# The first weight chunk is loaded ahead of the first full load of x, and each of the next three one x load earlier

## The chip, the core and the metric

One NeuronCore of a Trainium2 chip runs the whole program. The metric is the device time of one execution in microseconds; lower is better. TensorE multiplies, VectorE and ScalarE work on tiles, GpSimd (POOL) takes some of the elementwise work, and SP's queue issues nearly all transfers between HBM and the on-chip memory.

## The reference

Three steps follow each other on 2 x 3008 tokens of 256 features. All of it is computed to float32 accuracy.

```python
X = np.fft.fft(np.fft.fft(x, axis=1), axis=2).real      # x: 2, 3008, 256
h = X.reshape(6016, 256) @ w_in                         # 256 x 2048, float64
x = np.maximum(h, 0.0) ** 2 @ w_out                     # 2048 x 256
h = x @ w2_in
P = a[0] + a[1]*h + a[2]*h**2 + a[3]*h**3
Q = 1.0 + abs(b[0])*abs(h) + abs(b[1])*h**2
out = P / (Q + 1e-6) @ w2_out
```

## The kernel before

**The Fourier stage.** The length 3008 is split as 64 x 47. A first transform of length 47 runs on TensorE from x, which comes in ten loads: load 0 is a small one on ACT's queue (`x0`), loads 1 to 7 are two transfers of 384 KB each on SP's queue, loads 8 and 9 one transfer each (`X_CH`, `x_load`, L234). `u_mm` (L246) multiplies a load with the constant `c47`, in two halves of the feature axis. Each half goes through the load's first transfer and then through its second. ScalarE copies one half, VectorE adds and subtracts, and the result is the tile U (`u_copy`, `u_out`). When all ten loads are in U, `f_d` and `f_s` transform on (with the constants `cd` and `r0`), and ScalarE and VectorE split the result into x1h and x1l, the high and low parts of a tile of tokens. There are four slots for loads of x (`xt`).

**The weights.** Each layer has 16 chunks of weights. A chunk of the first layer comes as raw float64 words in two transfers of 256 KB (`w_load`, L328). ScalarE takes an absolute value (L337), VectorE puts the float32 together in four steps (L340 to L354), then sums and differences (L361), ScalarE rounds to the high part (L369) and VectorE subtracts to get the low part (L374). Then the first layer's product `h1` can use the chunk. A single row of weights, `w0`, is loaded, split and placed by small steps of its own (L379 to L406).

**The layers.** Twelve tiles of 384 or 512 tokens go through layer one (h1, the relu square, o1) and layer two (h2, the rational function, o2). Each product is three passes of high and low parts. Tiles 0 and 1 go through layer one side by side (`ORDER1`), while their chunks are still being made; from then on tiles follow one another. In the first microseconds and in the Fourier stage some multiplies of zeros (`hot`, L282) run on TensorE for its clock.

**The order of the work.** Every step is entered into a planner, `Queues`, with an engine, an assumed cost, a place, what it needs and which slots it takes. The planner then goes through time: among all steps that are ready it takes the one with the smallest key, and the order that it finds is the program's order on every engine.

```python
rank = (start, op["place"], op["n"])                                         # L110
...
place = -32 + c
...
add(("x", c), "SP" if c else "ACT", 0.54 * n if c else 0.5, place if c else -50, lambda c=c: x_load(c), take=("xt",),
    lat=X_LAT if c > 1 else 4.0 if c else 5.0,
    after=[("wd", W_FIRST[c] - 1)] if W_FIRST[c] else [])                    # L291
...
add(("wd", j), "SP", 1.5, place - 4, lambda j=j, w=w: w_load(j, *w), take=(raw,), lat=DMA_LAT,
    after=([("wd", j - 1)] if j else []) + [("x", c) for c in range(NC) if c < NC and W_FIRST[c] <= j])   # L427
```

`W_FIRST[c]` is the number of weight chunks that stand before load c of x: load c is issued after chunk `W_FIRST[c] - 1`, and chunk j after all loads with `W_FIRST[c] <= j`. Three more steps on SP's queue are tied to loads of x: `w0` is loaded after load 1 and placed after load 6, and `cd` and `r0` have a place (`C_AT`, -21.12) behind the loads of x (-31 and on) and before the chunks (-8 and on), but wait for nothing. `c47` is issued ahead of everything.

Of the kernel before, what the change touches and what calls it, by code (L numbers as in the profile page):

```python
# [52 lines left out]
AB_AT = 0  # L53
W_TAGS = (("g2", "x2h", "g2", "x2l"), ("g2",))
W2_AT, W2_STEP = 6.94, 1.11
W_FIRST, SPILL_W = (0, 0, 1, 1, 2, 2, 3, 3, 4, 4), 16


def f32(ap):
# [962 lines left out]
```

## Time and profile before

| | us |
|---|---|
| runs of the kernel before | 1092.48, 1089.34, 1089.12 (median 1089.34) |
| the profiled execution, its time | 1088.24 |
| its span, first to last instruction | 1086.3 |
| TensorE busy | 1053.5 (97% of the span) |
| VectorE busy | 1009.5 (93%) |
| ScalarE busy | 987.5 (91%) |
| GpSimd busy | 491.7 (45%) |
| mean granted clock of TensorE | 0.996 |

The profile is one execution; its time is the span and 1.9 us around it. Busy shares are means over stages with different limits, so the first 60 us have to be read by themselves. SP's rows are issues of transfers: a transfer's landing is its issue plus the time to landing that the view of transfers gives.

### The profile page before, as it was taken

How to read it: one execution, taken by the hardware profiler on the slowest of the kernel's cores; microseconds unless marked ns; L12 is line 12 of the kernel's file. 1: busy time of each engine (PE TensorE's matmuls, PEld its weight loads, DVE VectorE, ACT ScalarE, POOL GpSimd, SP SyncE). 2: the span in 40 equal slices, each digit the busy share in tenths (PEclk: the TensorE clock that was granted, in tenths of full speed). 3: DMA queues.
4: the chain of work that ended last, by engine and by line, in shares of the span. 5: the costliest groups of instructions: out<-in, count | busy, mean ns of one | idle time of the engine just before them, and what ended most of it. 6: DMA issues, size and time to landing. Idle time of an engine off the chain costs nothing.

```text
span 1086.3 us, 21308 instructions
## 1 busy us (share of the span) xinstructions
PE 1053.5 (97%) x7692; PEld 992.0 (91%) x7692; DVE 1009.5 (93%) x1806; ACT 987.5 (91%) x2009; POOL 491.7 (45%) x373
## 2 busy tenths in 40 slices
PE   9999989999999999999999999999999999999986
PEld 9899978899999999989899989999999999999985
DVE  5999999999899999999899899999899999899997
ACT  3888989999999999989999999999999999999896
POOL 0000015455444555445555545545545555545476
PEclk9999999999999999999999999999999999999999
DMA  9654400000000000000000000000000000000000
GB/s 333 207 204 127 136 1 1 25 2 11 11 11 11 6 16 11 1 21 11 2 21 11 1 21 11 1 21 11 1 21 10 2 11 11 2 11 11 2 11 20
DMA packets 26837, 36.81 MB, mean 34 GB/s; under 512 B 2315, under 2 KB 19341, under 8 KB 26733
## 3 DMA queue, kind: packets, MB, share of 16 engines
q1 hardware_dynamic: 26477, 34.94, 9.6%
q8 instruction: 61, 1.00, 0.4%
q10 hardware_dynamic: 256, 0.52, 0.2%
q14 instruction: 43, 0.35, 0.1%
HBM read 26.65 MB, written 8.78 MB: 33 GB/s over the span
## 4 chain that ended last, share of the span: by engine, by line
PE 51%; ACT 28%; DVE 13%; issue 6%; DMA 2%; POOL 1%; SPq 0%; ACTq 0%; POOLq 0%; DVEq 0%
PE o2a L672 13%; PE p L613 9%; PE o1a L672 6%; PE o1b L672 6%; PE p L644 4%; ACT y L761 4%; PE o2b L613 3%; ACT t L738 3%; ACT g L700 3%; ACT g L706 3%; ACT u L748 3%; ACT y L765 3%; ACT u L733 2%; DVE p L784 2%; ACT g L710 2%
## 5 line engine op out<-in xcount | busy, mean ns | idle before, releaser
L795 POOL TENSOR_TENSOR g<-t,y 128x512 fp32r<-128x512 f32 (+1 forms) x182 | 249.9, 1373 | 423.2 <-DVE t L791 194.8
L715 POOL TENSOR_TENSOR g<-g,g 128x512 fp32r<-128x512 f32 x160 | 211.6, 1323 | 153.8 <-ACT g L710 105.4
L672 PE MATMUL o2a<-g,w2hi 128*128 128x256 f32 (+1 forms) x1440 | 262.8, 283 | 6.8 <-POOL g L795 6.7
L672 PEld LDWEIGHTS o2a<-g,w2hi 128*128 128x128 f32 x1440 | 212.0, 189 | 13.9 <-POOL g L795 9.4
L778 DVE SCALAR_TENSOR_TENSOR g<-t,ab,y 128x512 fp32r<-128x512 f32 (+1 forms) x177 | 137.4, 778 | 13.1 <-ACT y L765 12.0
L672 PE MATMUL o2a<-g,w2lo 128*128 128x256 f32 (+1 forms) x720 | 145.1, 281 | 0.0
L672 PE MATMUL o1a<-g,w1hi 128*128 128x512 f32 x352 | 140.1, 398 | 1.6 <-POOL g L715 1.6
L672 PE MATMUL o1b<-g,w1hi 128*128 128x512 f32 x352 | 138.8, 394 | 0.0
L784 DVE SCALAR_TENSOR_TENSOR p<-u,g 128x512 f32<-128x512 f32 (+2 forms) x178 | 133.3, 749 | 0.7
L791 DVE SCALAR_TENSOR_TENSOR t<-t,ab,p 128x512 f32<-128x512 f32 (+2 forms) x178 | 129.2, 726 | 1.1
L748 ACT ACTIVATE u<-u 128x512 f32<-128x512 f32 (+2 forms) x178 | 110.3, 620 | 13.1 <-DVE u L744 12.3
L613 PE MATMUL p<-x2h,w2hi 128*128 128x256 f32 (+1 forms) x534 | 109.5, 286 | 8.4 <-DVE x1h L789 3.9
L765 ACT ACTIVATE y<-y 128x512 f32<-128x512 f32 (+1 forms) x185 | 115.2, 624 | 1.6
L761 ACT ACTIVATE y<-u 128x512 f32<-128x512 f32 (+1 forms) x177 | 109.6, 620 | 7.4 <-POOL g L795 3.7
L744 DVE SCALAR_TENSOR_TENSOR u<-u,ab,p 128x512 f32<-128x512 f32 (+1 forms) x134 | 97.1, 725 | 19.9 <-ACT t L738 18.9
L700 ACT ACTIVATE g<-g 128x512 f32<-128x512 f32 x160 | 101.2, 633 | 12.9 <-DVE g L690 12.5
L706 ACT ACTIVATE g<-g 128x512 fp32r<-128x512 f32 (+1 forms) x175 | 109.7, 627 | 3.3 <-PE o1b L672 1.9
L672 PEld LDWEIGHTS o2a<-g,w2lo 128*128 128x128 f32 x720 | 111.0, 190 | 0.0
L710 ACT ACTIVATE g<-g 128x512 f32<-128x512 f32 (+1 forms) x175 | 109.6, 626 | 1.2
L613 PE MATMUL p<-x2h,w2lo 128*128 128x256 f32 (+1 forms) x534 | 107.2, 282 | 0.0
L613 PE MATMUL p<-x2l,w2hi 128*128 128x256 f32 (+1 forms) x534 | 107.2, 282 | 0.0
L690 DVE TENSOR_TENSOR g<-p,bc 128x256 f32<-128x256 f32 x238 | 96.6, 417 | 5.5 <-ACT bc L680 3.3
(263 smaller groups left out, 2875.8 us busy)
## 6 DMA issues: line engine op xcount, KB each, us to landing
g<-in_dram SPq DMA_DIRECT2D x48, 256.0 KB, 3.5
xt<-in_dram SPq DMA_DIRECT2D x15, 384.0 KB, 5.8
out_dram<-os SPq DMA_DIRECT2D x21, 256.0 KB, 2.1
udram<-U SPq DMA_DIRECT2D x4, 640.0 KB, 5.3
ut<-udram SPq DMA_DIRECT2D x10, 256.0 KB, 3.0
x2h<-in_dram SPq DMA_DIRECT2D x8, 256.0 KB, 5.2
x2l<-in_dram SPq DMA_DIRECT2D x8, 256.0 KB, 4.4
xt<-in_dram ACTq DMA_DIRECT2D x1, 384.0 KB, 4.8
```

What stands on the lines that cost most here:

```text
L613: nc.tensor.matmul(h[:, c * n:(c + 1) * n], l[:, k, :], r[:, k], start=(q == 0), stop=(q == 5))
L672: nc.tensor.matmul(O[t][e], l[:, e * 128:(e + 1) * 128], r[:, c * n:(c + 1) * n], start=(i == 0 and q == 0 and not one), stop=(i == NF - 1 ...
L700: nc.scalar.activation(out=e["g"], in_=e["g"], func=ACTF.Relu)
L706: nc.scalar.activation(out=e["gh"], in_=e["g"], func=ACTF.Square)
L710: nc.scalar.activation(out=e["g"], in_=e["g"], func=ACTF.Square)
L715: eng.tensor_tensor(out=e["gl"], in0=e["g"], in1=f32(e["gh"]), op=ALU.subtract)
L748: nc.scalar.activation(out=w, in_=w, func=ACTF.Abs)
L761: nc.scalar.activation(out=e["z"], in_=e["w"], func=ACTF.Abs_reciprocal_sqrt, bias=Q1)
L765: nc.scalar.activation(out=z, in_=z, func=ACTF.Square)
L778: nc.vector.scalar_tensor_tensor(out=e["gh"], in0=e["t1"], scalar=a0, in1=e["z"], op0=ALU.add, op1=ALU.mult)
L784: nc.vector.scalar_tensor_tensor(out=e["m"], in0=e["w"], scalar=Q1, in1=f32(e["gh"]), op0=ALU.add, op1=ALU.mult)
L795: nc.gpsimd.tensor_tensor(out=e["gl"], in0=e["t1"], in1=e["z"], op=ALU.mult)
```

## The change

One tuple is edited: the entries of loads 1, 3, 5 and 7 go up by one chunk.

```diff
-W_FIRST, SPILL_W = (0, 0, 1, 1, 2, 2, 3, 3, 4, 4), 16
+W_FIRST, SPILL_W = (0, 1, 1, 2, 2, 3, 3, 4, 4, 4), 16
```

Before, the ties say: loads 0, 1, chunk 0, loads 2, 3, chunk 1, loads 4, 5, chunk 2, loads 6, 7, chunk 3, loads 8, 9, then the other chunks. After, they say: load 0, chunk 0, loads 1, 2, chunk 1, loads 3, 4, chunk 2, loads 5, 6, chunk 3, loads 7, 8, 9, then the other chunks. The planner makes the order of all engines anew from these ties.

## Rows read from the trace of the kernel before

**Rows 1.** The page's table of engines: busy us, share, instructions.
```profile
PE 1053.5 (97%) x7692; PEld 992.0 (91%) x7692; DVE 1009.5 (93%) x1806; ACT 987.5 (91%) x2009; POOL 491.7 (45%) x373
```

**Rows 2.** Stretches: length, busy us (instructions) by engine, TensorE's granted clock, DMA share, GB/s.
```profile
core 0: us, PE busy (x) PEld busy (x) DVE busy (x) ACT busy (x) POOL busy (x), PEclk, DMA share, GB/s
...
8.00:34.00 26.00, 24.58 (x191) 23.92 (x189) 21.97 (x59) 11.30 (x26) 0.00 (x0) 1.00 1.02 363
42.00:56.00 14.00, 12.61 (x93) 11.94 (x92) 13.44 (x35) 12.76 (x36) 0.00 (x0) 1.00 0.29 93
56.00:120.00 64.00, 63.97 (x462) 61.20 (x462) 60.38 (x131) 54.55 (x115) 0.00 (x0) 1.00 0.51 166
```

**Rows 3.** TensorE's waits, 33 to 62 us: total, times, longest.
```profile
PE p L490 <- DVE U L273: 1.3, 1, 1.3
PE p L626 <- ACT y L697: 0.7, 1, 0.7
PE p L626 <- DVE x1l L543: 0.7, 1, 0.7
```

**Rows 4.** Timeline of TensorE: start, us, line, form, count, idle before.
```profile
6.78 1.06 PE L251 MATMUL o1b<-c_t,xt 96*128 96x96 f32 x8
...
11.03 0.59 PE L255 MATMUL p<-c_t,xt 128*128 128x188 f32 x2
...
17.44 0.51 PE L255 MATMUL o2a<-c_t,xt 128*128 128x188 f32 x2
...
20.50 0.51 PE L255 MATMUL p<-c_t,xt 128*128 128x188 f32 x2
...
33.60 0.44 PE L490 MATMUL p<-cd_t,U 128*66 128x130 f32 x2 [1.29 <-DVE U L273]
...
41.97 0.36 PE L626 MATMUL p<-x1h,w1hi 128*128 128x256 f32 x1
```

**Rows 5.** Timeline of SP's queue: start and length of each issue, transfers.
```profile
1.19 0.89 SPq L244 DMA_DIRECT2D xt<-in_dram  x2
...
2.60 0.42 SPq L209 DMA_DIRECT2D cd_t<-in_dram  x1
3.07 0.57 SPq L209 DMA_DIRECT2D r_t<-in_dram  x1
3.68 0.66 SPq L330 DMA_DIRECT2D g<-in_dram  x1
5.50 0.34 SPq L332 DMA_DIRECT2D g<-in_dram  x1
...
13.97 0.33 SPq L332 DMA_DIRECT2D g<-in_dram  x1
```

**Rows 6.** The chain that ended last, in order of time, first pieces: start, us.
```profile
0.74 4.75 DMA xt<-in_dram
5.50 0.34 SPq L332
5.89 5.09 DMA xt<-in_dram
```

**Rows 7.** Transfers issued around 1.9, 3.2, 5.6 and 14 us: KB, us to landing.
```profile
xt<-in_dram SPq DMA_DIRECT2D x1, 384.0 KB, 5.8
...
cd_t<-in_dram SPq DMA_DIRECT2D x1, 257.0 KB, 5.7
r_t<-in_dram SPq DMA_DIRECT2D x1, 66.0 KB
...
g<-in_dram SPq DMA_DIRECT2D x1, 256.0 KB, 4.5
...
g<-in_dram SPq DMA_DIRECT2D x1, 256.0 KB, 8.3
```

**Rows 8.** Timeline of VectorE: its first step on w0, its first on chunk 0.
```profile
8.06 0.21 DVE L392 TENSOR_SCALAR cw<-cw 16x128 f32<-16x128 f32 x1 [7.07 <-ACT cw L383]
...
10.73 0.43 DVE L340 TENSOR_SCALAR cw<-cw 128x512 f32<-128x512 f32 x1 [0.56 <-ACT cw L337]
```

**Rows 9.** Timeline of TensorE, 140 to 151 us: the end of its longest wait.
```profile
144.26 0.61 PE L613 MATMUL p<-x2h,w2hi 128*128 128x384 f32 x2 [2.15 <-DVE t L756]
```

**Rows 10.** Stretch behind that wait, with columns as in rows 2.
```profile
144.00:150.00 6.00, 5.74 (x21) 4.98 (x22) 5.53 (x11) 5.35 (x14) 0.84 (x1) 0.72 0.02 4
```

## The prediction

> **What bounds the kernel now.** I read the page's table of engines first: TensorE is busy 1053.5 of 1086.3 us [rows 1], so over the whole span it is the engine to keep fed, and a change at the start pays only through the moment at which TensorE gets its work and through the holes it has later. The table by stretch tells the stages apart [rows 2]. From 8 to 34 us the 16 DMA engines are full (share 1.02, 363 GB/s), TensorE is busy for 24.58 of 26 us, and VectorE for 21.97, so that it is idle for 26.00 - 21.97 = 4.03 us. From 42 to 56 us the DMA has little to do (share 0.29), VectorE is full (13.44 of 14), and TensorE lacks 14.00 - 12.61 = 1.39 us. From 56 to 120 us TensorE lacks nothing (63.97 of 64).
>
> So the start is a DMA stage in which TensorE is paced by x, followed by a short stage in which VectorE, turning float64 weights into pairs, leaves small holes on TensorE. The table of waits names these: when U is complete TensorE waits 1.3 us for VectorE's last U, and later 0.7 us for ScalarE's y and 0.7 us for VectorE's x1l [rows 3].
>
> The timeline of TensorE shows how close the race of x is [rows 4]: load 0 is finished at 6.78 + 1.06 = 7.84 us, load 2 starts at 11.03, and later one load takes 20.50 - 17.44 = 3.06 us, with no hole between load 4 and load 5. The transform of U starts at 33.60 and the first h1 at 41.97.
>
> **The change part by part.** Only the order of SP's queue is edited, through the planner. Its key is (start, place). With the edit the only loads free at zero are those of the constants, so the planner takes cd and r0 before anything else; then chunk 0 (freed by load 0 on ACT's queue), x load 1, w0, x load 2, chunk 1, loads 3 and 4, chunk 2, loads 5 and 6, the placing of w0, chunk 3, loads 7, 8, 9, chunk 4. No instruction is added or removed. In front of x load 1 come four transfers that were behind it: cd, r0 and the two halves of chunk 0. Later chunk 1 passes load 3, chunk 2 load 5, chunk 3 load 7, two transfers each. From load 8 on the bytes in front of every transfer are as before.
>
> *Issue.* The four took SP 0.42 + 0.57 + 0.66 + 0.34 = 1.99 us [rows 5]. Load 1 was issued from 1.19, so it is now issued from about 3.2. Before, the ninth transfer (chunk 0's second half) was held until 5.50 us, and the chain shows load 0's landing (0.74 + 4.75 = 5.49) in front of it [rows 5, 6]: eight are outstanding at most. Chunk 0 and load 1 are now all within the first eight, and w0 (16 KB) becomes the ninth, issued after 5.50; its steps on VectorE, at 8.06 before [rows 8], come a few us later, into VectorE's idle time. I cost issue and w0 at nothing, since the full DMA engines hide both; without that cover the cost would be 1.99 us, which is less than the next term and inside it.
>
> *Load 1's data.* cd and r0 are 257 + 66 KB and chunk 0 is 2 x 256 KB [rows 7]: 855 kB, 2.36 us at 363 GB/s. Load 1's second half was issued at about 1.19 + 0.45 = 1.64 and took 5.8 us [rows 5, 7]: landed at 7.4, now 9.8. The same number comes from other rows: chunk 0's second half landed at 5.50 + 4.5 = 10.0 with the same bytes in front of it [rows 5, 7]. I take 9.9. The first half of load 1, 393 kB or 1.08 us earlier, lands near 8.8. TensorE, done with load 0 at 7.84, therefore stands for about 1.0 us, runs a quarter of load 1 (0.76 us), waits for the second half, and finishes load 1 at 9.9 + 0.75 x 3.06 = 12.2. Load 2 is at its old place in bytes (first half landed at 5.89 + 5.09 = 10.98 [rows 6]), so it is there, and starts at 12.2 instead of 11.03: **1.2 us late**.
>
> *Later loads.* With no hole left load 5 would start at 20.50 + 1.2 = 21.7 and want its second half at 22.5. That half now stands where chunk 2's second half stood, which landed at 13.97 + 8.3 = 22.27 [rows 5, 7]. It just fits; with a slip as large as one chunk's transfer (524 kB, 1.44 us) the delay would be 2.6. Loads 3 and 7 make the same swap, with TensorE late by as much. So U is complete 1.2 us later (bounds 0.9, if load 1 gains on the other transfers, and 2.6).
>
> *Chunks.* Chunk 0 lands earlier by load 1, which leaves its front: 786 kB, 2.2 us; chunks 1, 2 and 3 likewise by one load each. VectorE started chunk 0 at 10.73 [rows 8] and can now start near 8.5, when it has nothing of U. By the end of U it is ahead by 2.2 us, and by 1.2 more because U is late. What this can give on TensorE is bounded: by the 1.39 us of holes from 42 to 56 us above, by nothing below, since the order on VectorE is fixed beforehand and x1l, not a chunk, ends one of the two waits. I take half, **0.7 us**. ScalarE's step on chunk 0 now stands before its copy of load 0; nothing needs that copy's bank before load 3, and the cost is nothing, or 0.7 us at most if a copy of a later load were held.
>
> *The way from U to h1*, 41.97 - 33.60 = 8.4 us, has idle multiplies for the clock and ScalarE's and VectorE's chunk steps in it; I let it stay as it is.
>
> *Everything after* is re-planned. No row shows the new order. What it can be worth is bounded by the largest hole in the trace: before 144.26 us TensorE stood for 2.15 us behind VectorE's t [rows 9], and its granted clock over 144 to 150 us was 0.72, which is (1 - 0.72) x 6 = 1.7 us lost at the lower of the two levels, 1.2 GHz [rows 10]. Such a hole more or less is worth 2.15 + 1.7 = 3.85 us either way. Between these ends I take zero: the order of tiles in the steady part is chained by hand and stays.
>
> Sum: +1.2 - 0.7 = +0.5 us, a span of 1086.8 and 1088.7 for an execution like the profiled one (1088.24). That execution was 1.1 us below the median of the runs shown, 1089.34, so against the median: **1089.9 us**.
>
> *A rule against the change.* The holes that the change makes, 1.0 us near 8 us and a short one near 9.6, are smaller than the 2.15 us hole that was followed by the lower clock, and the holes of [rows 3] were followed by none (1.00 granted from 42 to 120 us [rows 2]); by these rows the sum stays at 1089.9. The Trainium skill, TensorE: Matmul & The Clock Gate, section "HAM oscillation — how this bites in real kernels", says that a matmul stage that waits for DMA loads may restart throttled after each wait. By that rule load 1 and what follows it would run at half speed for a while, which is the first rival.
>
> **The rivals.** *The clock falls at the start.* For it: the hole waits for a DMA with little work of TensorE before it; against it: it is half the hole of [rows 9]. It costs the 1.7 us of [rows 10]: 1089.9 + 1.7 = 1091.6, still no difference that can be told. *A new hole at a later handover* is the case on the slower side: the re-planned order makes TensorE wait once more as before 144.26, long enough that the clock follows. It decides once hole and clock together exceed 2.8 us; a whole one gives 1089.9 + 3.85 = 1093.7. For it speaks that VectorE has little slack (13.44 of 14 [rows 2]) and its order is static; against it that 56 to 120 us has no hole at all. *The hole before 144.26 vanishes*, because another order serves VectorE's t sooner: 1089.9 - 3.85 = 1086.0, faster by 0.3%. Nothing in the rows ties that hole to the weights of the start. *The change does not reach the end*: TensorE absorbs the delay in the holes up to 56 us (1.3 + 0.7 + 0.7 [rows 3]), 1089.3; against it, the 1.3 is a wait for U itself and moves with it.
>
> **How the numbers follow.** Some 0.3%, 3.3 us, can be told from no change here. Chances: the forecast, with delays from 0.9 to 2.6 and gains from 0 to 1.39 (1088.8 to 1091.9), 0.55; absorbed 0.13; clock at the start 0.10; new hole 0.14; vanished hole 0.08. Of the vanished hole some 0.05 ends beyond 0.3%, of the new hole 0.13, and 0.01 of the clock with the 2.6 us delay. Faster 0.05, same 0.81, slower 0.14. The range 1087.0 to 1093.5 leaves out about 0.07 below and 0.10 above.
>
> **What would show it.** Right: load 1 landing near 9.9, a hole of about 1 us on TensorE before it, load 2 at about 12.2, U's transform at about 34.8, the first h1 at about 43.2, chunk 0's first VectorE step before 9.5, holes from 42 to 56 us smaller than 1.39. Wrong: load 2 after 13.5 us or TensorE granted 1.2 GHz before 20 us (then the start was under-priced); a shift at 120 us that differs from the one at the end by more than 2 us (then the re-planned order, not the loads, made the time).

## The result, and the profile after

| | before | after |
|---|---|---|
| median of four runs, us | 1089.23 | 1098.42 |
| lowest to highest | 1087.76 to 1092.48 | 1096.38 to 1100.37 |
| the profiled execution: time, span | 1088.24, 1086.3 | 1100.37, 1098.6 |

The ratio is 1.0079, with a 95% interval of 1.0056 to 1.0102. The change costs 0.8%, some 9 us; the forecast of 1089.9 was wrong, and its range ended at 1093.5. The profiled execution of after is the slowest of its four, so the trace below shows 12.3 us of span where the medians show 9.2.

The page's table of engines, as in [rows 1]. The instructions are the same in number; TensorE is busy 8.7 us longer for them, at a mean granted clock of 0.985 where it was 0.996, and the rest of the 12.3 us is idle time.

```profile
PE 1062.2 (97%) x7692; PEld 1003.0 (91%) x7692; DVE 1012.5 (92%) x1806; ACT 985.4 (90%) x2009; POOL 492.8 (45%) x373
```

After's timeline of SP's queue (start and length of each issue), which answers to [rows 5]. The four transfers stand in front of load 1 as the prediction had them, load 1 is issued at 3.47, and w0 is the one that is held, to 5.44.

```profile
2.13 0.66 SPq L330 DMA_DIRECT2D g<-in_dram  x1
2.83 0.59 SPq L332 DMA_DIRECT2D g<-in_dram  x1
3.47 1.10 SPq L244 DMA_DIRECT2D xt<-in_dram  x2
5.44 0.33 SPq L379 DMA_DIRECT2D g<-in_dram  x1
```

After's timeline of TensorE, which answers to [rows 4] and, below 200 us, to nothing that before has. A hole of 1.08 us stands before load 1 at 8.86; load 2 starts at 14.88 (before 11.03), U's transform at 36.81 (33.60), h1 at 46.85 (41.97).

```profile
8.86 0.99 PE L255 MATMUL o2a<-c_t,xt 128*128 128x188 f32 x2 [1.08 <-DMA xt<-in_dram]
...
14.88 0.67 PE L255 MATMUL p<-c_t,xt 128*128 128x188 f32 x2
...
36.81 0.44 PE L490 MATMUL p<-cd_t,U 128*66 128x130 f32 x2 [0.83 <-DVE U L273]
...
40.27 4.23 PE L282 MATMUL p<-hot_t 128*128 128x128 f32 x24
...
46.85 0.36 PE L626 MATMUL p<-x1h,w1hi 128*128 128x256 f32 x1
...
213.77 0.58 PE L644 MATMUL p<-x1h,w1hi 128*128 128x256 f32 x1 [1.93 <-ACT v L505]
...
232.93 0.47 PE L613 MATMUL p<-x2h,w2hi 128*128 128x256 f32 x2 [1.44 <-DVE g L690]
```

After's stretches, with the columns of [rows 2]. From 8 to 16 us the granted clock was 0.57, so it stood at 1.2 GHz for about (1 - 0.57) x 8 / 0.5 = 6.9 us. From 213 to 237, around the two late holes, it was 0.79, about 10 us at the lower level.

```profile
8.00:16.00 8.00, 7.14 (x32) 7.15 (x33) 5.13 (x18) 3.44 (x8) 0.00 (x0) 0.57 1.04 389
...
213.00:237.00 24.00, 21.16 (x117) 19.55 (x118) 16.19 (x31) 20.42 (x43) 9.89 (x8) 0.79 0.08 28
```

So two things that the prediction named as signs of its being wrong are there: load 2 after 13.5 us, and 1.2 GHz before 20 us. Whether they made the time is for the experiments. To follow a shift through the kernel I use ScalarE's first write of x2h (L721) for a tile, the end of its layer one. Before, tiles 0, 1 and 2:

```profile
131.08 0.48 ACT L721 ACTIVATE x2h<-o2a 128x384 fp32r<-128x384 f32 x1
...
165.48 0.59 ACT L721 ACTIVATE x2h<-o1a 128x512 fp32r<-128x512 f32 x1
...
250.90 0.58 ACT L721 ACTIVATE x2h<-o1a 128x512 fp32r<-128x512 f32 x1
```

After, the same tiles:

```profile
136.10 0.47 ACT L721 ACTIVATE x2h<-o2a 128x384 fp32r<-128x384 f32 x1
...
166.93 0.58 ACT L721 ACTIVATE x2h<-o1a 128x512 fp32r<-128x512 f32 x1
...
261.90 0.58 ACT L721 ACTIVATE x2h<-o1a 128x512 fp32r<-128x512 f32 x1
```

After is late by 3.2 us at U, 4.9 at h1, 5.0 at tile 0, 11.0 at tile 2, and still by 11.1 at tile 11 (1025.77 against 1014.72). From about 390 us on every engine's order is the same in both kernels. The whole loss thus comes in two pieces, one up to h1 and one between tile 0 and tile 2, and 1.2 us more in the last tile. The second piece is not a steady loss: at tile 1 after is only 1.5 us late, so its order first brings tile 1's layer one forward by 3.6 us, and then loses 9.6 us between tile 1 and tile 2.

### The profile page after: what moved, and what is told of

The parts are those of the page before. It is cut to its first block, busy times and chain, and to the rows that moved or that the text cites. A ratio compares the mean times of both kernels' runs of the same rounds, so it can differ in the third digit from the quotient of the medians.

```text
span 1098.6 us, 21299 instructions
## 1 busy us (share of the span) xinstructions
PE 1062.2 (97%) x7692; PEld 1003.0 (91%) x7692; DVE 1012.5 (92%) x1806; ACT 985.4 (90%) x2009; POOL 492.8 (45%) x373
## 2 busy tenths in 40 slices
DMA packets 26837, 36.81 MB, mean 34 GB/s; under 512 B 2315, under 2 KB 19341, under 8 KB 26733
## 4 chain that ended last, share of the span: by engine, by line
PE 55%; ACT 22%; DVE 16%; issue 5%; POOL 1%; DMA 1%; SPq 0%; DVEq 0%; ACTq 0%; POOLq 0%
PE o2a L672 14%; PE p L613 11%; PE o1a L672 7%; PE o1b L672 7%; PE p L644 5%; PE o2b L613 3%; ACT y L761 3%; ACT g L706 3%; ACT t L738 2%; ACT y L765 2%; ACT g L700 2%; ACT u L748 2%; ACT u L733 2%; PE o2b L644 2%; DVE p L784 2%
## 5 line engine op out<-in xcount | busy, mean ns | idle before, releaser
L672 PEld LDWEIGHTS o2a<-g,w2hi 128*128 128x128 f32 x1440 | 213.6, 191 | 13.5 <-POOL g L795 8.7
L778 DVE SCALAR_TENSOR_TENSOR g<-t,ab,y 128x512 fp32r<-128x512 f32 (+1 forms) x177 | 141.4, 800 | 17.2 <-ACT y L765 12.4
L613 PE MATMUL p<-x2h,w2hi 128*128 128x256 f32 (+1 forms) x550 | 113.6, 288 | 8.3 <-DVE t L756 3.1
L744 DVE SCALAR_TENSOR_TENSOR u<-u,ab,p 128x512 f32<-128x512 f32 (+2 forms) x139 | 100.8, 725 | 18.0 <-ACT t L738 16.9
L613 PE MATMUL p<-x2h,w2lo 128*128 128x256 f32 (+1 forms) x550 | 111.4, 284 | 0.0
L613 PE MATMUL p<-x2l,w2hi 128*128 128x256 f32 (+1 forms) x550 | 111.4, 284 | 0.0
L690 DVE TENSOR_TENSOR g<-p,bc 128x256 f32<-128x256 f32 x246 | 99.0, 416 | 9.8 <-ACT bc L680 7.0
```

Of the source, the lines that this page charges most:

```text
L613: nc.tensor.matmul(h[:, c * n:(c + 1) * n], l[:, k, :], r[:, k], start=(q == 0), stop=(q == 5))
L672: nc.tensor.matmul(O[t][e], l[:, e * 128:(e + 1) * 128], r[:, c * n:(c + 1) * n], start=(i == 0 and q == 0 and not one), stop=(i == NF - 1 ...
L778: nc.vector.scalar_tensor_tensor(out=e["gh"], in0=e["t1"], scalar=a0, in1=e["z"], op0=ALU.add, op1=ALU.mult)
```

## The experiments

The theories. **A, the loads**: load 1 is late, the clock falls, and what follows is late. **B, the plan**: the planner, given other ties, writes another order for VectorE, ScalarE and TensorE, and this order is what costs, early, late or in both places. The expectations, written one by one, divide B further: in E1 to E4 theory B is the order between 140 and 260 us alone and theory C the order as a whole, and P and Q (E6, E7) are its early and its later part. Each ratio is against runs of the kernel before that were made beside it on the same chip; their medians were 1088.36 us beside E1 to E4, 1089.43 beside E5 to E8 and 1088.64 beside E9 to E12. Line numbers in the traces of the experiments are up to 19 higher for the added lines.

| kernel | median us (runs) | ratio, 95% | U | h1 | tile 0 | tile 0 to tile 2 |
|---|---|---|---|---|---|---|
| before | 1089.23 (4) | | 33.60 | 41.97 | 131.08 | 119.82 |
| after | 1098.42 (4) | 1.0079, 1.0056 to 1.0102 | 36.81 | 46.85 | 136.10 | 125.80 |
| E1 loads only | 1090.02 (10) | 1.0018, 1.0006 to 1.0029 | 34.65 | 43.02 | 132.17 | 119.80 |
| E2 plan only | 1098.40 (4) | 1.0098, 1.0081 to 1.0114 | 37.95 | 48.12 | 137.43 | 122.80 |
| E3 hole filled | 1096.85 (4) | 1.0075, 1.0058 to 1.0092 | 36.87 | 48.36 | 137.66 | 123.88 |
| E4 chunk 0 only | 1090.28 (10) | 1.0023, 1.0014 to 1.0033 | 35.80 | 43.06 | 134.27 | 119.41 |
| E5 chunks 1 to 3 only | 1097.90 (4) | 1.0070, 1.0046 to 1.0093 | 37.45 | 48.22 | 142.32 | 118.03 |
| E6 late order only | 1097.03 (4) | 1.0074, 1.0050 to 1.0097 | 34.12 | 45.97 | 135.27 | 123.90 |
| E7 early order only | 1092.75 (6) | 1.0035, 1.0022 to 1.0047 | 36.41 | 45.67 | 134.42 | 119.90 |
| E8 table load early | 1096.93 (4) | 1.0072, 1.0054 to 1.0090 | 35.26 | 45.30 | 134.62 | 122.81 |
| E9 after's order to tile 0 | 1093.61 (4) | 1.0048, 1.0030 to 1.0066 | 36.85 | 45.82 | 135.12 | 120.06 |
| E10 after's order from tile 0 | 1098.48 (4) | 1.0094, 1.0076 to 1.0112 | 33.76 | 42.12 | 134.27 | 127.21 |
| E11 after, no zero batches | 1096.78 (4) | 1.0082, 1.0062 to 1.0102 | 36.34 | 46.02 | 136.04 | 122.84 |
| E12 before, no zero batches | 1087.35 (10) | 0.9998, 0.9982 to 1.0014 | 33.91 | 41.71 | 130.06 | 119.69 |

Columns U, h1 and tile 0 are the starts, in each profiled execution, of U's transform, the first h1 and tile 0's x2h; the last column is the time from tile 0's x2h to tile 2's. In the profiled executions of E5 and E9 TensorE ran at half speed up to about 13 us, though neither has a hole there (the first eight rows of load 0 take 1.99 us where before has 1.10), so what these two lose at the start is not their order alone.

**E1 and E2: the loads alone, the plan alone.** The planner runs on the ties of before (E1) or of after (E2); then its first 17 steps on SP's queue, which issue the transfers, are put into the other kernel's order, and nothing else moves.

```diff
+        spots = [i for i, o in enumerate(order) if o[3] in SP_ORDER]
+        moved = {order[i][3]: order[i] for i in spots}
+        for i, key in zip(spots, SP_ORDER):
+            order[i] = moved[key]
```

> All engines keep the plan of the kernel before; only the first 17 steps of SP's queue stand in the order of the changed kernel. Theory A (the loads: load 1 comes late, TensorE stands about 1 us, its clock falls) expects the whole loss at the start: U's transform 3 us later than before (near 36.8), h1 4 to 5 us later, and the end 4 to 9 us later, 1093 to 1098 us. Theory B (the re-planned order makes the loss between 140 and 260 us) expects the start's 3 to 5 us and nothing more after 140 us: 1092 to 1094 us. Theory C (only the re-planned order matters) expects 1089 us.

> All engines have the plan of the changed kernel; only the first 17 steps of SP's queue stand in the order of before, so load 1 is first again. Theory A expects no hole before load 1, no low clock near 9 us and the time of before, 1089 us. Theory B expects U's transform near 33.6 to 34.6 us and 5 to 6 us lost between 140 and 260 us: 1094 to 1096 us. Theory C expects 1098 us.

E1's timeline of TensorE:

```profile
9.02 0.59 PE L263 MATMUL o2a<-c_t,xt 128*128 128x188 f32 x2 [1.22 <-DMA xt<-in_dram]
...
12.41 0.51 PE L263 MATMUL p<-c_t,xt 128*128 128x188 f32 x2
...
34.65 0.44 PE L498 MATMUL p<-cd_t,U 128*66 128x130 f32 x2 [1.29 <-DVE U L281]
```

The change of the loads is what the prediction said: a hole of 1.2 us, load 2 at 12.41 (forecast 12.2), U late by 1.05 us (forecast 1.2). That shift stays (tile 0 +1.1, tile 2 +1.1, span +1.1) and gives 0.18%. E2 has before's transfers in before's order and is as slow as after. So B holds and A explains a small part. The narrower theory B of the expectation fell: with U's transform at 37.95, E2 is late at the start already. Its row says what is late there:

```profile
37.95 0.70 PE L498 MATMUL p<-cd_t,U 128*66 128x130 f32 x2 [3.49 <-DVE U L281]
```

TensorE has done its loads and waits 3.49 us for VectorE's U, where before it waited 1.3 [rows 3]. It was through its loads at 37.95 - 3.49 = 34.46, which is 2.15 us later than before although the transfers are before's: a hole of 1.50 us behind VectorE's U, at 33.81, is in that.

**E3: after, with the hole filled.** Four multiplies of zeros stand on TensorE in front of load 1.

```diff
+        at = [o[3] for o in order].index(("um", 1, 0))
...
+    queues.fill = lambda: hot(4, "p0")
```

> The changed kernel with four multiplies of zeros (about 1.1 us at the full clock) on TensorE between load 0 and load 1, and no other change of any order. Theory A expects the granted clock to stay at its upper level from 8 to 15 us, U's transform 2 to 3.4 us earlier than in the changed kernel (near 34 to 35), and the end 3 us earlier or more: 1092 to 1096 us. If the clock falls all the same, or the later loads bind, the start stays at 36.8 and the time at 1098. Theory C expects 1098.

E3's stretch from 8 to 16 us and its transform of U:

```profile
8.00:16.00 8.00, 7.80 (x61) 7.46 (x60) 4.83 (x17) 3.42 (x8) 0.00 (x0) 1.00 1.04 393
```
```profile
36.87 0.44 PE L492 MATMUL p<-cd_t,U 128*66 128x130 f32 x2 [3.19 <-DVE U L275]
```

The clock is at its higher level, TensorE is through its loads by 36.87 - 3.19 = 33.68, and U's transform starts where it did in after, 36.81. E11 below, which has after's order up to 40 us, kept the upper level without any filling, with a hole as long:

```profile
8.80 0.59 PE L255 MATMUL o2a<-c_t,xt 128*128 128x188 f32 x2 [1.13 <-DMA xt<-in_dram]
...
36.34 0.44 PE L490 MATMUL p<-cd_t,U 128*66 128x130 f32 x2 [3.14 <-DVE U L273]
```

By these two executions the lower clock at the start of after cost half a microsecond at U at most: TensorE was slow inside a wait for VectorE. The time (1.0075) is not distinguishable from after's.

**E4 and E5: one part of the tuple each.**

```diff
-W_FIRST, SPILL_W = (0, 0, 1, 1, 2, 2, 3, 3, 4, 4), 16
+W_FIRST, SPILL_W = (0, 1, 1, 1, 2, 2, 3, 3, 4, 4), 16   # E4
+W_FIRST, SPILL_W = (0, 0, 1, 2, 2, 3, 3, 4, 4, 4), 16   # E5
```

> Chunk 0 alone stands in front of load 1; chunks 1 to 3 have their old places after loads 3, 5 and 7. The planner makes the order anew. Theory A expects the same hole before load 1, the same fall of the clock and 3 us or more lost at the start: 1092 to 1098 us. Theory B cannot say what the new order does after 140 us, but expects the shift there to be another one than in the changed kernel.

> Chunk 0 stays behind load 1 as before; chunks 1 to 3 stand one load of x earlier, as in the changed kernel. The planner makes the order anew. No hole before load 1 and no low clock near 9 us. If the change's loss came with chunk 0's place, the time is that of before, 1088 to 1091 us; if any new plan of this kind loses, 1093 us or more.

E4 puts chunk 0 in front of load 1, has the hole (1.07 us) and a granted clock of 0.79 from 8 to 16 us, and loses 0.23%, less than the 1092 us or more that theory A expected. E5 leaves load 1 in its place, has no such hole (the half speed near 9 us was not expected), and loses 0.70%, but elsewhere than after: its tile 0 is 11.2 us late, and from tile 0 to tile 2 it takes 118.03, less than before. Each tuple gives a plan of its own with losses in its own places; no chunk's place has a price that carries over.

**E6 and E7, E9 and E10: which part of the order.** Two plans are made, one on each set of ties, and joined: the steps that the one plan starts before a cut, then the other plan's remaining steps in its order. The cut is the first step of U's transform (E6: before's order, then after's; E7 the reverse) or tile 0's x2h (E9: after's order, then before's; E10 the reverse; these two also keep the buffers that the first plan chose).

```diff
+        cut = next(o[0] for o in early if o[3] == ("fm", 0, 0))      # E9, E10: ("xh", 0)
+        head = [o for o in early if o[0] < cut]
+        keys = {o[3] for o in head}
+        return [o[2] for o in head + [o for o in late if o[3] not in keys]]
```

> The steps that the planner of the kernel before puts ahead of U's transform stand in that order (loads included); every later step stands in the order of the changed kernel's plan. Theory P (the early order on VectorE and ScalarE makes the loss: U and h1 late by 3 to 5 us) expects h1 near 42 and the time of before, 1088 to 1090 us. Theory Q (the later order makes at least half of it, between 140 and 260 us) expects h1 near 42 and 3 to 6 us lost after 140 us: 1091 to 1095 us.

> The reverse: early steps in the order of the changed kernel, every step from U's transform on in the order of before. Theory P expects U's transform near 36.8, h1 4 to 5 us late and that shift to stay to the end: 1092 to 1095 us. Theory Q expects the same start but less than half of the loss: 1090 to 1093 us. If early and late order only fail together, both spliced kernels are near 1089.

> All steps that the changed kernel's plan puts ahead of the first write of x2h (the end of layer one of tile 0, at 131 us before) stand in its order, and the buffers chosen there; every later step stands in the order of before. If the loss is made in two places, the start (to h1) and the handover (140 to 260 us), this kernel keeps the first alone: a shift of about 5 us at 131 us that stays to the end, 1093 to 1095 us. If the order of the first 130 us also makes the later holes, the shift grows to 9 us or more: 1098 us.

> The reverse: the order of before up to the first write of x2h, the changed kernel's order from there on. With the loss in two places: no shift at 131 us, then 3 to 6 us lost between 140 and 260 us: 1092 to 1095 us. If the early order makes the later holes: 1089 us.

E7, the early order alone, costs 0.35%, and E6, all the rest, 0.74%, more than its expectation allowed, since h1 came at 45.97 and not near 42. E9 shows that after's order up to tile 0 costs 0.48% and E10 that the order from there on costs 0.94%. E10's figure is too large for that part alone: it has a hole of 4.44 us at the joint, at 136.19, that after has not, was late by 3.2 us at tile 0, where no shift was expected, and its 1098.48 lies above the 1095 that was expected at most. The parts do not add up exactly, since an order written for one start is run behind another. What is the same throughout is the last column of the table, for the twelve kernels made of these two orders. From tile 0 to tile 2 the kernels with before's late order (before, E1, E7, E9, E12) take 119.7 to 120.1 us, and those with after's take at least 122.8. The whole stretch, before, E2 and after:

```profile
131.08:250.90 119.82, 113.47 (x717) 103.40 (x716) 114.54 (x216) 110.35 (x231) 50.58 (x41) 0.99 0.02 7
```
```profile
137.43:260.23 122.80, 111.40 (x714) 102.28 (x713) 112.35 (x206) 109.09 (x231) 49.31 (x40) 1.00 0.02 6
```
```profile
136.10:261.90 125.80, 115.16 (x709) 106.01 (x708) 111.05 (x206) 109.18 (x230) 48.89 (x40) 0.96 0.02 6
```

E2 has the full clock there and TensorE stands idle for 122.80 - 111.40 = 11.4 us, against 6.4 before. E8 and E11, at full clock too, take 122.81 and 122.84. So the order itself costs 3.0 us, also against E1, which has before's order there at the full clock (119.80). These 3.0 are the balance of 3.6 us gained up to tile 1 (30.83 in E2, 34.40 before) and 6.6 lost behind it (91.97 and 85.42). After takes 3.0 more at a granted clock of 0.96: the lower clock behind its holes at 213.77 and 232.93. That second part differs between executions: after's own four had mean granted clocks of 0.985, 0.988, 0.990 and 0.993 with spans of 1098.6, 1097.7, 1095.5 and 1094.6 us. The holes do not: E8 at full clock has the same two, and before has neither.

```profile
212.29 0.38 PE L646 MATMUL p<-x1h,w1hi 128*128 128x256 f32 x1 [1.93 <-ACT v L507]
...
229.37 0.48 PE L615 MATMUL p<-x2h,w2hi 128*128 128x256 f32 x2 [1.45 <-DVE g L692]
```

**E8: ScalarE's table load.** After's plan puts chunk 0's step first on ScalarE. After's timeline of ScalarE:

```profile
7.91 1.28 ACT L337 ACT_TABLE_LOAD   x1 [7.91 <-DMA g<-in_dram]
9.20 0.67 ACT L337 ACTIVATE cw<-g 128x512 f32<-128x512 f32 x1
```

Before, the first rows of ScalarE after its issue of load 0 were these:

```profile
1.19 1.28 ACT L383 ACT_TABLE_LOAD   x1 [1.19 <-PEq L1009]
7.71 0.32 ACT L383 ACTIVATE cw<-g 16x128 f32<-16x128 f32 x1 [5.25 <-DMA g<-in_dram]
```

The table load stands at the first activation. Where that one was w0's, it ran at 1.19, ahead of the wait for w0's data, in idle time; where it is chunk 0's, it runs only at 7.91, behind a wait for a transfer, and chunk 0's step waits 1.28 us for it. The two differ in what is waited for: w0 comes in one transfer, chunk 0 in two. That this is why the load stands behind a wait in after is likely, and no run tests it. E8 is after with one small copy on ScalarE (the zero tile, written once more with zeros) right behind the issue of load 0.

```diff
+        at = [o[3] for o in order].index(("x", 0)) + 1
...
+    queues.table = lambda: nc.scalar.activation(out=zero, in_=hot_t, func=ACTF.Copy)
```

> The changed kernel with one small copy on ScalarE right after the issue of load 0, so that the load of its table (1.28 us) no longer stands between the landing of chunk 0 and its first step. If VectorE's chain of chunk steps sets U, then its first step on chunk 0 comes 1.2 us sooner (near 8.7) and U's transform 0.5 to 1.3 us sooner, near 35.6 to 36.3: 1096 to 1098 us. If TensorE or the loads set U, U's transform stays at 36.8 and the time at 1098.

E8's timeline of ScalarE and of TensorE:

```profile
1.19 1.28 ACT L919 ACT_TABLE_LOAD   x1 [1.19 <-PEq L1012]
8.08 0.66 ACT L339 ACTIVATE cw<-g 128x512 f32<-128x512 f32 x1 [5.29 <-DMA g<-in_dram]
```
```profile
35.26 0.44 PE L492 MATMUL p<-cd_t,U 128*66 128x130 f32 x2 [1.81 <-DVE U L275]
```

Chunk 0's step comes 1.1 us sooner and U's transform 1.55 us sooner than in after, a little more than expected (35.26, expected 35.6 at the earliest); the lead is 1.48 us still at tile 0. The medians, 1098.42 and 1096.93, differ by as much, but their intervals overlap.

**E11 and E12: no zero batches between U and h1.** In after the two batches of zero multiplies stand together (24 rows, two for each multiply, 40.27 to 44.50, in part at the lower clock) where before they stand apart (12 from 36.79, 12 from 39.31). Both kernels leave them out; the result does not use them.

```diff
+        return [o[2] for o in order if o[3][:2] != ("hot", 0)]
```

> The changed kernel without the two batches of six zero multiplies that stand between U's transform and h1 (they took 4.23 us in one piece, 40.27 to 44.50). Everything else keeps its order. If these batches delay h1, then h1 is 2 to 4 us sooner (43 to 45 in place of 46.85) and the end 2 to 4 us sooner: 1094 to 1096 us. If TensorE only waits there for ScalarE and VectorE, or if its clock then stays low, h1 stays within 1 us.

> The kernel before without the same two batches (1.60 and 1.56 us there, apart from each other). If they delay h1 there too, h1 is 0.5 to 1.5 us sooner than 41.97 and the end as much: 1087.5 to 1089 us. If they lie beside ScalarE's and VectorE's steps, h1 stays; if the clock falls for want of them, the time rises by 1 to 3 us.

E11's timeline of TensorE and its stretch from 38 to 48 us:

```profile
41.73 0.80 PE L519 MATMUL p<-cd_t,v 128*128 128x128 f32 x2 [1.28 <-ACT v L505]
...
46.02 0.56 PE L626 MATMUL p<-x1h,w1hi 128*128 128x256 f32 x1
```
```profile
38.00:48.00 10.00, 8.70 (x40) 8.41 (x40) 8.38 (x22) 7.78 (x27) 0.00 (x0) 0.51 0.38 122
```

Without the batches h1 comes only 0.8 us earlier, 0.5 of which E11 has at U already: TensorE then waits for ScalarE's v, and the clock stays at 1.2 GHz for nearly the whole stretch. With the clock low, E11 alone cannot say what the doubled batch costs. E9 helps: it has after's order here with the doubled batch, at a granted clock of 1.00 from U to h1:

```profile
39.75 3.25 PE L301 MATMUL p<-hot_t 128*128 128x128 f32 x24
...
45.82 0.36 PE L645 MATMUL p<-x1h,w1hi 128*128 128x256 f32 x1 [0.59 <-ACT v L524]
```

The batch takes 3.25 us there and not 4.23, and behind it TensorE still waits 0.59 us for v, so the batch by itself does not set h1. E12 shows no difference (0.9998), so it is no better version either.

## Why the prediction was wrong, by its own steps

**Issue and load 1's data: right.** The first half of load 1 landed at 3.47 + 5.34 = 8.81 by the chain of after, forecast 8.8; the hole was 1.08 us, forecast 1.0.

```profile
3.47 5.34 DMA xt<-in_dram
```

In E1 this made U 1.05 us late, forecast 1.2, within the bounds of 0.9 and 2.6. The sum's last step, 1089.34 + 0.5, is 1089.84 and not 1089.9; nothing hangs on it.

**The rule against the change.** The prediction argued that a hole smaller than the 2.15 us of [rows 9] would leave the clock alone. After's 1.08 us hole was followed by 0.57 from 8 to 16 us, so that argument failed, and the rival "the clock falls at the start" came true. Its price of 1.7 us did not: E3 takes the low clock away and U does not come earlier, and E11, without the low clock, has U 0.5 us earlier. The Trainium skill, TensorE: Matmul & The Clock Gate, section "HAM oscillation — how this bites in real kernels", has stages that wait for loads restart throttled. After agrees; E11, with the same order up to there and a hole of 1.13 us, was granted 1.00 from 8 to 16 us, and so was E1 with 1.22 us, so here the rule holds in one execution and not in another.

**Chunks: wrong, -0.7 measured as no gain.** The data of chunk 0 came earlier, but the step went from data to VectorE without asking what ScalarE's row in between needs. VectorE started chunk 0 at 9.90, forecast 8.5 and before 10.73, and its first low part (L374) came at 15.02, against 14.75 before. After's timeline of VectorE:

```profile
9.90 0.43 DVE L340 TENSOR_SCALAR cw<-cw 128x512 f32<-128x512 f32 x1 [8.90 <-ACT cw L337]
...
15.02 0.42 DVE L374 TENSOR_TENSOR w1lo<-eo,w1hi 128x256 fp32r<-128x256 f32 x1 [0.48 <-ACT w1hi L369]
...
35.52 0.42 DVE L340 TENSOR_SCALAR cw<-cw 128x512 f32<-128x512 f32 x1
...
36.11 0.42 DVE L344 TENSOR_SCALAR cw<-cw 128x512 uint32<-128x512 uint32 x1
36.45 0.30 DVE L273 TENSOR_TENSOR U<-g,o1b 128x94 f32<-128x94 f32 x1
36.61 0.68 DVE L349 SCALAR_TENSOR_TENSOR cw<-g,cw 128x512 uint32<-128x512 uint32 x1
37.21 0.30 DVE L273 TENSOR_TENSOR U<-g,o1b 128x94 f32<-128x94 f32 x1
```

The last rows show the other side: three steps of a chunk stand between the last adds of U, which TensorE is waiting for. In before the steps of that chunk, the fifth in both kernels, began behind the last add:

```profile
33.60 0.32 DVE L273 TENSOR_TENSOR U<-g,o1b 128x94 f32<-128x94 f32 x1
33.76 0.42 DVE L340 TENSOR_SCALAR cw<-cw 128x512 f32<-128x512 f32 x1
```

What the planner takes to be ready sooner is put sooner into VectorE's fixed order, and here in front of U. E3 splits after's 3.2 us at U: TensorE is through its loads 33.68 - (33.60 - 1.29) = 1.4 us later than before, and the wait for VectorE grows from 1.29 to 3.19, 1.9 us. In E8 that wait is 1.81, so 1.4 of the 1.9 go with the table load. The split holds for after's transfers only: with before's transfers (E2) the same order makes U late by 4.35 us.

**The way from U to h1: wrong.** It was left as it is; it took 10.0 us instead of 8.4 (E2 10.2, E8 10.0, E1 8.4). The granted clock there was 0.83 in after, 0.75 in E2, 0.83 in E8 and 1.00 in before and E1. E9, with after's order at 1.00, took 9.0. So some 0.6 us of the 1.7 is the order, and some 1.1 goes with the clock. Why the clock fell there in after is open: its wait for U just before, 0.83 us, is shorter than the 1.29 of before, behind which it did not fall.

**"Everything after is re-planned ... I take zero": the step that failed.** Its bounds of 3.85 us either way were one hole of the trace, as if the plan could only gain or lose a single one. Between tile 0 and tile 2 after's order has several: 3.0 us at full clock, which the bounds still held, and 6.0 with the lower clock of the profiled execution, which they did not; and the early part of the order (at U and from U to h1) comes on top. E2, the new order without the new transfers, measures the whole of what was put at zero: 0.98%, some 10 us, where the transfers that the sum priced cost 0.18% (E1). The sign by which the prediction said it would know this, a shift that grows by more than 2 us after 120 us, is there: +5.0 at tile 0, +12.3 at the end. Zero was chosen since the order of tiles is chained by hand; but within a tile the places of VectorE's and ScalarE's steps are the planner's, and it changed them up to about 390 us.

The nearest rival, "a new hole at a later handover" (1093.7), has the right kind of cause and less than half of the 9.2 us.

Adding up the profiled execution: to U +3.2 (about 1.4 loads and 1.9 order, by E3), U to h1 +1.7 (0.6 order, 1.1 clock, by E9), h1 to tile 0 +0.1, to tile 2 +3.0 for the order and +3.0 for the clock, the last tile and the end +1.2 (the order is before's there, the granted clock 0.92 where it was 0.96), in all 12.2 of 12.3.

**Open.** Which step of the later order opens the holes at 213.77 and 232.93 was not tried; E6, E9 and E10 only show in which part of the order they lie. Nor did the runs tie the planner's other choice to a single tie: E4 and E5 show that it is not additive. No run beat the kernel before by more than can be told.

## What to carry to other kernels

Where a planner writes the order, an edit of its input is two changes, the one intended and a new order for every engine; run them apart (old order with the new transfers, new order with the old ones) before reading anything into the sum. A price for "re-planned" should be bounded by all holes that the static order could open at the handovers, not by the largest one now, and set towards slower when the present order has few. And before counting data that lands earlier as a gain, follow it through each engine's next instruction, the one-time work that stands in front of it included.

## What was not expected of the hardware

ScalarE's table load (1.28 us) ran at 1.19 us in before and at 7.91 in after, behind a wait for a transfer that the first activation needs. The Trainium skill, ScalarE: Activation LUTs, section "Step-by-step: what each stage is for", says that the compiler places it right before the activation that needs it; the traces agree. They also show that it can stand behind a wait for that activation's data (after) or ahead of it (before, where w0's activation waited until 7.71), and that one small activation at the start brings it back to 1.19 (E8).

Much smaller holes than the 2.15 us of [rows 9] went with a fall of TensorE's clock, and not each time: 1.08 us in after with 6.9 us at 1.2 GHz, 1.13 us in E11 and 1.22 us in E1 with none. The same two holes around 213 and 233 us were followed by about 10 us at the lower level in after and by none in E2 and E8, which share its order there; from tile 0 to tile 2 after took 3.0 us longer than they did.
